# Batch 1's k turned by one DMA transpose instead of 64 PE transposes

## The chip, the core and the metric

The kernel runs on one core of a Trainium2 chip. The metric is the device time of one execution in microseconds, taken as the median of several runs. The core has five engines with a queue each, which run side by side and wait for one another through semaphores: TensorE (PE, with the weight loads PEld shown apart), VectorE (DVE), ScalarE (ACT), GpSimd (POOL) and SyncE (SP). POOL and SP also issue the DMA transfers; the 16 DMA engines work through POOL's transfers in a queue that the profile calls q0 and through SP's in one called q1.

## What is computed

An attention with 4 batches, 8 heads, 768 positions and head size 64, followed by a gated feed-forward layer with a gated residual. Each position attends to the positions closer than 16, and to one summary of each of the 24 blocks of 32 positions (the block's maximum of k and its mean of v).

```python
k_sum = k.reshape(B, H, nb, block, D).max(axis=3)
v_sum = v.reshape(B, H, nb, block, D).mean(axis=3)
scores_l = scale * q @ k.T, kept where abs(i - j) < window
scores_s = scale * einsum('bhsd,bhnd->bhsn', q, k_sum) + log(block)
a = softmax(concatenate([scores_l, scores_s]))
x = a @ concatenate([v, v_sum])            # then heads side by side: 3072 x 512
ffn = (gelu(x @ w_gate) * (x @ w_val)) @ w_out
out = x + sigmoid(x @ w_res) * ffn
```

## The kernel before

**Units.** The 3072 rows of x are worked through in eight units `u` of 384 rows: `u // 2` is the batch, `u % 2` its half. A unit's feed-forward part makes twelve tiles `gvT[:, fo]` (`fo` 0 to 11): four products into `g` with `w_gate`, four into `vv` with `w_val`, a gelu on ACT (L400) and a product on DVE (L401). Then `first_out` (unit 0) or `mid_out` weaves the output products `r` (L433) and `f` (L443) of unit u with the attention of unit u+1: `s_step` makes the scores of one head pair (L317) and their exponentials, `av_step` the weighted sum of v (L355), and `xt_step` or `xt_dma` turn the result for the next unit. The order of all instructions is written out by hand; each engine runs its own in that order.

**Layouts.** `s_step` wants k with the head dimension on the partitions: `kW[b % 2]` holds, for each of twelve 64-row tiles and four head pairs, 128 columns: 64 own keys, 32 keys of the neighbouring tiles (the rims, columns `QT:BAND`), and the 24 block maxima (`BAND:BAND + NB`). `k_blocks` makes the maxima (L237) and copies them to all tiles (L241) on DVE. `k_rims` copies the rims (L245, L246) on the engine that it is given. The two `kW` buffers alternate by batch.

**How k gets there.** Batches 0 and 1 are loaded by `load_k` into `k_sb` with eight positions to a row (long contiguous pieces), turned by 64 PE transposes into PSUM (`turn_pair`, L220), and placed by `k_place`: an ACT copy (L252), then `k_blocks` and `k_rims` on DVE, head pair by head pair. For batch 1 the load is issued on POOL's queue before unit 0's loop goes on, the transposes (`turn_all`) stand after fo 0 of unit 1, and the four `k_place` after fo 0, 2, 4 and 6. Batches 2 and 3 are loaded by `load_k_nat` into `k_nat` (one transfer for each head, 64 partitions by 12 tiles by 64 values), turned by a single DMA transpose on SP's queue (`turn_k`, L131) at fo 6 of the even unit before, with `k_rims` on POOL just behind it; `k_blocks` follow on DVE at fo 2 to 5 of the odd unit.

**What else stands on the queues there.** POOL, after the weights: the load of batch 1's k, eight loads of its v (`vext`, L107), six of its q (`q_nat`, L127). A load of POOL waits until the eighth load before it has landed. In unit 1 at fo 5, `turn_q` turns q by two DMA transposes on SP (L136), and `vsum_grp` makes the block means of v: PE products `vs` (L290), an ACT copy `vpart` (L294), four small transfers `vsum` issued by POOL (L296). Then POOL copies them to six of the twelve tiles with `vsum_bc` (L302, twice), and to the others in `mid_out`. SP has the three outputs of unit 0 (L456), the rims of v (`v_rims`, L113 and L114), the two q transposes, and later the `xt_dma` and outputs of unit 1.

In unit 0 the four `xt_step` take turns between two PSUM banks and are all copied out by ACT (L382); the fourth is `xt_step(0, 3, st, **o_turn)`.

Of the kernel before, what the change touches and what calls it, by code (L numbers as in the profile page):

```python
# [15 lines left out]
def kernel(  # L16
# [11 lines left out]
    nc = tc.nc  # L28
# [16 lines left out]
    NP = H // 2  # L45
# [15 lines left out]
    ps_o = ctx.enter_context(tc.tile_pool(name="ps_o", bufs=1, space=bass.MemoryType.PSUM))  # L61
# [25 lines left out]
    def load_k(b, t, i, n):  # L87
        hs = slice(i * H // n, (i + 1) * H // n)
        nc.gpsimd.dma_start(out=t[:, hs].rearrange("p h j d -> p h (j d)"),
                            in_=k[b, hs].rearrange("h (p j) d -> p h (j d)", j=PJ))  # L90

    def k_tile():
        return qk.tile([PP, H, PJ, D], BF16, tag="k_sb", name="k_sb")
# [11 lines left out]
    def v_loads(b):  # L105
        for h in range(H):
            nc.gpsimd.dma_start(out=vext[b % 2][0:QT, :, h, 0:D],  # L107
                                in_=v[b, h].rearrange("(t p) d -> p t d", p=QT))
# [7 lines left out]
    k_sb, q_sb = {}, {}  # L116

    def load_k_nat(b):
        k_nat = qk.tile([QT, NT, DM], BF16, tag="k_nat", name="k_nat")
        for h in range(H):  # L120
            nc.gpsimd.dma_start(out=k_nat[:, :, h * D:(h + 1) * D],
                                in_=k[b, h].rearrange("(t p) d -> p t d", p=QT))
        return k_nat

    def load_q_nat(b):
        for c in range(NQ):
            nc.gpsimd.dma_start(out=q_nat[:, c].rearrange("p (h d) -> p h d", d=D),  # L127
                                in_=q[b, :, c * 128:(c + 1) * 128, :].rearrange("h p d -> p h d"))

    def turn_k(b, k_nat):  # L130
        nc.sync.dma_start_transpose(out=kW[b % 2].rearrange("d t g k -> d (t g) k")[:, :, 0:QT],  # L131
                                    in_=k_nat.rearrange("p t f -> p (t f)"))
# [6 lines left out]
    with tc.manual_schedule():  # L139
# [76 lines left out]
        def turn_pair(src, hp, tp):  # L216
            n, _, nj, _ = src.shape
            for j in range(nj):
                for hh in range(2):
                    nc.tensor.transpose(tp[hh * 64:hh * 64 + 64, j, :], src[:, 2 * hp + hh, j, :],  # L220
                                        ident[0:n, 0:n])
            return tp

        def turn_tile(src, pool, tag):
            return pool.tile([128, src.shape[2], src.shape[0]], BF16, tag=tag, name="tp")

        def turn_all(src):
            n, _, nj, _ = src.shape
            s2 = ps_s.tile([128, 2, 1024], BF16, tag="s", name="tp")
            tps = [s2[:, i, 0:nj * n].rearrange("d (j p) -> d j p", j=nj) for i in range(2)]  # L230
            tps += [turn_tile(src, ps_t, "t"), turn_tile(src, ps_o, "ao")]
            return [turn_pair(src, hp, tps[hp]) for hp in range(NP)]

        def k_blocks(b, hp):
            kw = kW[b % 2][:, :, hp]
            ks = work.tile([128, NB], BF16, tag="ks", name="ks")
            nc.vector.tensor_reduce(  # L237
                out=ks.rearrange("d (t n) -> d t n", n=2),
                in_=kw[:, :, 0:QT].rearrange("d t (n w) -> d t n w", w=BLK),
                axis=mybir.AxisListType.X, op=ALU.max)  # L240
            nc.vector.tensor_copy(kw[:, :, BAND:BAND + NB], ks.unsqueeze(1).to_broadcast([128, NT, NB]))  # L241

        def k_rims(b, hps, eng):
            kw = kW[b % 2][:, :, hps]
            eng.tensor_copy(kw[:, 0:NT - 1, :, QT:QT + WIN], kw[:, 1:NT, :, 0:WIN])  # L245
            eng.tensor_copy(kw[:, 1:NT, :, QT + WIN:BAND], kw[:, 0:NT - 1, :, QT - WIN:QT])  # L246
# [4 lines left out]
        def k_place(b, hp, tp):  # L251
            nc.scalar.copy(kW[b % 2][:, :, hp, 0:QT].rearrange("d t (p j) -> d t p j", j=PJ),  # L252
                           tp.rearrange("d j (t p) -> d t p j", t=NT))
            k_blocks(b, hp)
            k_rims(b, slice(hp, hp + 1), nc.vector)
# [121 lines left out]
        def xt_step(u, ko, st, pool, tag, copy=nc.vector.tensor_copy):  # L377
            xp = pool.tile([128, TU], BF16, tag=tag, name="xp")
            for sub in range(NSUB):
                nc.tensor.transpose(xp[:, sub * 128:(sub + 1) * 128],  # L380
                                    st["xn"][:, ko, sub, :], ident[:])
            copy(st["xT"][:, ko, :], xp[:])  # L382
# [5 lines left out]
        def new_unit():  # L388
            return {"xn": upool.tile([128, KO, NSUB, 128], BF16, tag="xn", name="xn"),
                    "xT": upool.tile([128, KO, TU], BF16, tag="xT", name="xT")}  # L390


        def gv_mm(ps, w, st, fo, kos):
            for ko in kos:
                nc.tensor.matmul(ps[:, 0:TU], w[:, ko, fo * 128:(fo + 1) * 128], st["xT"][:, ko, :],  # L395
                                 start=(ko == 0), stop=(ko == KO - 1), skip_group_check=True)
# [82 lines left out]
        tk, tq, ao = {}, {}, {}  # L479
# [11 lines left out]
        st = new_unit()  # L491
# [44 lines left out]
        o_turn = dict(pool=ps_o, tag="ao", copy=nc.scalar.copy)  # L536
# [6 lines left out]
        def gv_part(fo, ko):  # L543
            gv_mm(gv[fo][0], w_gate, st, fo, (ko,))
            gv_mm(gv[fo][1], w_val, st, fo, (ko,))
# [2 lines left out]
        xt_step(0, 2, st, **t_turn)  # L548
        gv_part(0, 1)
        gv_mm(gv[1][0], w_gate, st, 1, (0, 1))  # L550
        xt_step(0, 3, st, **o_turn)
        gv_part(0, 2)
        gv_mm(gv[1][1], w_val, st, 1, (0, 1))
        gv_part(0, 3)
# [100 lines left out]
        for u in range(NU):  # L655
            b, half = u // 2, u % 2
            nb = b + 1
            if half == 0 and nb == 1:
                k_sb[nb] = k_tile()
                load_k(nb, k_sb[nb], 0, 1)  # L660
                v_loads(nb)
                load_q_nat(nb)
            if u:
                gvT = upool.tile([128, FO, TU], BF16, tag="gvT", name="gvT")
            for fo in range(0 if u else 2, FO):
                if u == 0 and fo == 2:
                    unit0_extras(fo)
                    continue
                if u > 1 and fo == 0:
                    fo_first(st, gvT)  # L670
                elif u and fo == FO - 2:
                    fo_last_two(st, gvT)
                elif u == 0 or fo < FO - 2:
                    fo_step(st, gvT, fo)
                if u == 0:
                    unit0_extras(fo)
                if u == 0 and fo == 9:
                    tq = turn_all(q_sb[1])
                if u == 0 and fo in (9, 10):
                    for hp in range(2 * fo - 18, 2 * fo - 16):  # L680
                        q_place(1, hp, tq[hp])
                if half == 0 and 1 < nb < B and fo == 0:
                    pool_after(st["xT"][0:1, KO - 1, 0:1])
                    k_nat = load_k_nat(nb)
                    v_loads(nb)
                if half == 0 and b and fo == 1:
                    v_rims(b, HT, NT)
                if half == 0 and 1 < nb < B and fo == 6:
                    turn_k(nb, k_nat)
                    k_rims(nb, slice(0, NP), nc.gpsimd)  # L690
                if half == 1 and nb < B:
                    if fo == 0:
                        v_rims(nb, 0, HT)
                        if nb > 1:
                            pool_after(st["xT"][0:1, KO - 1, 0:1])
                            load_q_nat(nb)
                    if fo == (5 if nb == 1 else 1):
                        turn_q(nb, 0)
                        turn_q(nb, 1)
                        vsum_grp(nb, ps_t, "t")  # L700
                        for i in range(2):
                            vsum_bc(nb, 3 * i, 3 * i + 3, nc.gpsimd)
                    if nb == 1:
                        if fo == 0:
                            tk = turn_all(k_sb[nb])
                        if fo in (0, 2, 4, 6):
                            hp = (2, 0, 1, 3)[fo // 2]
                            k_place(nb, hp, tk[hp])
                    elif 2 <= fo < 2 + NP:
                        k_blocks(nb, fo - 2)  # L710
            if u == NU - 1:
                last_out(u, st, gvT)
            else:
                nst = new_unit()
                (mid_out if u else first_out)(u, st, gvT, nst)
                st = nst

# [29 lines left out]
```

The softmax here doesn't subtract the row's maximum and nothing guards it: scores larger than these inputs give would overflow.

## Time and profile before

| | |
|---|---|
| median of 3 runs | 256.26 us (256.26 to 256.71) |
| the profiled execution | 256.39 us, of which its span is 254.6 us |
| granted TensorE clock | 0.998 |
| 64 transposes of batch 1's k on PE (L220) | 207 ns each, overlapping, start 53.04 us |
| ACT copies of k out of PSUM (L252, all 8) | 798 ns each |
| DVE rim copies, one head pair (L245, L246, all 8 each) | 217 and 215 ns |
| POOL rim copies, all head pairs (L245, L246, 2 each) | 816 and 1096 ns |
| issue to landing: k_sb of batch 1 / kW<-k_nat | 18.6 us / 9.5 us |

The span is what the trace covers; the run's time also has what lies around it. A line of a timeline gives the start, the length, the engine, the line of the kernel, the operation with output and input, the count, and in brackets how long the engine had been idle and what ended that. The lines of a DMA queue give the packets, the megabytes and the time of its packets as a share of 16 engines' time.

### The profile page before, as it was taken

What the parts mean: (1) busy time and instruction counts of PE and PEld (TensorE: products, weight loads), DVE (VectorE), ACT (ScalarE), POOL (GpSimd) and SP (SyncE); (2) the same over time, 40 slices, a digit from 0 to 9 for tenths busy, and PEclk for the clock granted to TensorE, in tenths of its full rate; (3) what the DMA queues carried; (4) which work ended last, traced back from release to release, by engine and by line L of the source; (5) the groups of instructions that cost most, each with busy time, mean ns of one, the idle gap of its engine ahead of it and who ended that gap; (6) DMA issues with size and microseconds to landing.
All of it is one profiled execution on the core that took longest, in us unless ns stands there. A gap on an engine that the chain in (4) does not pass through costs nothing.

```text
span 254.6 us, 5847 instructions
## 1 busy us (share of the span) xinstructions
PE 246.6 (97%) x2303; PEld 139.7 (55%) x2328; DVE 159.4 (63%) x364; ACT 129.6 (51%) x216; POOL 97.3 (38%) x128
## 2 busy tenths in 40 slices
PE   6999999999999999999999999999999999999994
PEld 2676555565545665446544665446545555456544
DVE  6985796397667544858567544958567544854424
ACT  8885468366572337353572337254572337353320
POOL 8895542361506970274406970274404000000000
PEclk9999999999999999999999999999999999999999
DMA  5999999999404999399404999289604400230003
GB/s 80 177 182 197 197 205 207 175 176 222 61 19 121 159 150 150 56 161 171 103 18 120 162 155 153 49 162 170 104 18 115 98 3 0 50 139 0 3 1 124
DMA packets 98107, 29.34 MB, mean 115 GB/s; under 512 B 83224, under 2 KB 94944, under 8 KB 97984
## 3 DMA queue, kind: packets, MB, share of 16 engines
q0 software_dynamic: 68352, 14.76, 66.3%
q1 hardware_dynamic: 29728, 14.21, 25.7%
q8 instruction: 18, 0.29, 0.5%
q14 instruction: 9, 0.07, 0.1%
HBM read 29.36 MB, written 6.29 MB: 140 GB/s over the span
## 4 chain that ended last, share of the span: by engine, by line
PE 93%; DVE 5%; issue 2%; DVEq 0%
PE g L395 25%; PE vv L395 24%; PE f L443 23%; PE r L433 8%; PE s L317 3%; PE ao L355 3%; PE vs L282 1%; PE ao L367 1%; PE tp L220 1%; PE vs L290 1%; DVE ks L237 1%; PE xp L380 1%; DVE o L452 1%; DVE th L449 1%; PE gv L395 1%
## 5 line engine op out<-in xcount | busy, mean ns | idle before, releaser
L401 DVE TENSOR_TENSOR gvT<-ge,vv 128x384 bf16<-128x384 f32 x95 | 52.2, 552 | 48.1 <-PE vv L395 43.9
L400 ACT ACTIVATE ge<-g 128x384 f32<-128x384 f32 x95 | 46.7, 491 | 67.3 <-DVE gvT L401 34.8
L395 PE MATMUL g<-xT,w_gate 128*128 128x384 bf16 x380 | 78.0, 326 | 0.0
L395 PE MATMUL vv<-xT,w_val 128*128 128x384 bf16 x380 | 77.8, 326 | 0.0
L443 PE MATMUL f<-w_out,gvT 128*128 128x512 bf16 x262 | 62.7, 379 | 1.5 <-issue 1.1
L395 PEld LDWEIGHTS <-w_gate 128*128 128x128 bf16 x384 | 37.1, 98 | 26.2 <-issue 1.4
L395 PEld LDWEIGHTS <-w_val 128*128 128x128 bf16 x384 | 37.6, 98 | 24.7
L443 PEld LDWEIGHTS <-gvT 128*128 128x128 bf16 x276 | 25.7, 98 | 29.5
L107 POOL DMA_DIRECT2D vext<-in_v_dram x32 | 24.1, 777 | 15.0 <-DMA w_out<-in_moe_w_out_dram 5.6
L436 ACT ACTIVATE th<-r 128x512 f32<-128x512 f32 x24 | 13.5, 607 | 27.6 <-PE r L433 27.6
L449 DVE SCALAR_TENSOR_TENSOR th<-th,f 128x512 f32<-128x512 f32 (+2 forms) x26 | 16.6, 640 | 14.4 <-PE f L443 14.4
L341 DVE TENSOR_TENSOR P<-P,maskt 128x768 bf16<-128x768 bf16 x28 | 16.2, 580 | 11.0 <-ACT P L337 6.1
L433 PE MATMUL r<-w_res,xT 128*128 128x512 bf16 x88 | 22.7, 380 | 0.4
L302 POOL COPY vext<-vsum 32x1536 bf16<-32x1536 bf16 x12 | 17.2, 1464 | 13.0 <-DMA vsum<-vpart 12.9
L452 DVE SCALAR_TENSOR_TENSOR o<-th,xn 128x512 f32<-128x512 f32 (+2 forms) x26 | 18.2, 701 | 0.9
L375 DVE TENSOR_TENSOR xn<-ao,rz 128x384 bf16<-128x384 f32 x32 | 17.8, 557 | 1.1
L337 ACT ACTIVATE P<-s,bias_t 128x768 bf16<-128x768 f32 x17 | 15.3, 901 | 4.5 <-PE s L317 4.3
L127 POOL DMA_DIRECT2D q_nat<-in_q_dram x18 | 15.8, 899 | 0.9 <-issue 0.7
L334 ACT ACTIVATE P<-s,bias_t 128x384 bf16<-128x384 f32 x30 | 15.7, 579 | 0.0
L237 DVE TENSOR_REDUCE ks<-kW 128x24 bf16<-128x768 bf16 x16 | 15.1, 943 | 0.0
L433 PEld LDWEIGHTS <-xT 128*128 128x128 bf16 x96 | 8.8, 98 | 9.9
L373 DVE RECIPROCAL rz<-ao 128x6 f32<-128x6 f32 x32 | 6.1, 191 | 10.9 <-PE ao L355 10.0
(90 smaller groups left out, 187.1 us busy)
## 6 DMA issues: line engine op xcount, KB each, us to landing
out_dram<-o SPq DMA_DIRECT2D x23, 256.0 KB, 2.2
vext<-in_v_dram POOLq DMA_DIRECT2D x32, 96.0 KB, 6.4
q_nat<-in_q_dram POOLq DMA_DIRECT2D x18, 128.0 KB, 6.4
w_gate<-in_moe_w_gate_dram POOLq DMA_DIRECT2D x6, 256.0 KB, 8.9
w_val<-in_moe_w_val_dram POOLq DMA_DIRECT2D x6, 256.0 KB, 9.3
w_out<-in_moe_w_out_dram POOLq DMA_DIRECT2D x3, 512.0 KB, 14.4
k_nat<-in_k_dram POOLq DMA_DIRECT2D x16, 96.0 KB, 5.8
vext<-vext SPq DMA_DIRECT2D x6, 144.0 KB, 5.4
```

The lines of the kernel that those rows point to most:

```text
L107: nc.gpsimd.dma_start(out=vext[b % 2][0:QT, :, h, 0:D], in_=v[b, h].rearrange("(t p) d -> p t d", p=QT))
L237: nc.vector.tensor_reduce(out=ks.rearrange("d (t n) -> d t n", n=2), in_=kw[:, :, 0:QT].rearrange("d t (n w) -> d t n w", w=BLK), axis=myb ...
L302: eng.tensor_copy(vext[b % 2][96:128, lo:hi, :, 0:D], src)
L341: nc.vector.tensor_mul(Pf, Pf, maskt.unsqueeze(1).to_broadcast([128, 2 * HT, QT]))
L375: nc.vector.tensor_mul(xn, ao[:, :, :, 0:D], rz.to_broadcast([128, NSUB, 2, D]))
L395: nc.tensor.matmul(ps[:, 0:TU], w[:, ko, fo * 128:(fo + 1) * 128], st["xT"][:, ko, :], start=(ko == 0), stop=(ko == KO - 1), skip_group_ch ...
L400: nc.scalar.activation(ge[:], g[:, 0:TU], AF.Gelu)
L401: nc.vector.tensor_mul(gvT[:, fo, :], ge[:], vv[:, 0:TU])
L433: nc.tensor.matmul(r[:], st["xT"][:, ko, ss], w_res[:, ko, :], start=(ko == 0), stop=(ko == KO - 1))
L443: nc.tensor.matmul(st["f", sub][:], gvT[:, fo, ss], w_out[:, fo, :], start=(fo == 0), stop=(fo == FO - 1), skip_group_check=True)
L449: nc.vector.scalar_tensor_tensor(th[:, cs], th[:, cs], 1.0, f[:, 0:n], ALU.add, ALU.mult)
L452: nc.vector.scalar_tensor_tensor(o.rearrange("p (k d) -> p k d", d=128), th[:, cs].rearrange("p (k d) -> p k d", d=128), 0.5, x, ALU.mult, ...
```

## The change

Batch 1's k is loaded by `load_k_nat` and turned by `turn_k`, as batches 2 and 3 are. The turn is issued in unit 0, ahead of `first_out`. `k_rims` goes to POOL at fo 6 of unit 1, and the four `k_blocks` follow on DVE at fo 6 to 9. The last `xt_step` of unit 0 is copied out by DVE (the default of `copy`) and no longer by ACT.

```diff
-        xt_step(0, 3, st, **o_turn)
+        xt_step(0, 3, st, ps_o, "ao")
...
             if half == 0 and nb == 1:
-                k_sb[nb] = k_tile()
-                load_k(nb, k_sb[nb], 0, 1)
+                k_nat = load_k_nat(nb)
                 v_loads(nb)
                 load_q_nat(nb)
...
                         vsum_grp(nb, ps_t, "t")
                         for i in range(2):
                             vsum_bc(nb, 3 * i, 3 * i + 3, nc.gpsimd)
-                    if nb == 1:
-                        if fo == 0:
-                            tk = turn_all(k_sb[nb])
-                        if fo in (0, 2, 4, 6):
-                            hp = (2, 0, 1, 3)[fo // 2]
-                            k_place(nb, hp, tk[hp])
-                    elif 2 <= fo < 2 + NP:
-                        k_blocks(nb, fo - 2)
+                    lead = 6 if nb == 1 else 2
+                    if nb == 1 and fo == lead:
+                        k_rims(nb, slice(0, NP), nc.gpsimd)
+                    if lead <= fo < lead + NP:
+                        k_blocks(nb, fo - lead)
...
                 nst = new_unit()
+                if u == 0:
+                    turn_k(nb, k_nat)
                 (mid_out if u else first_out)(u, st, gvT, nst)
```

The functions that it now calls for batch 1, as they were:

```python
def load_k_nat(b):
    k_nat = qk.tile([QT, NT, DM], BF16, tag="k_nat", name="k_nat")
    for h in range(H):
        nc.gpsimd.dma_start(out=k_nat[:, :, h * D:(h + 1) * D],
                            in_=k[b, h].rearrange("(t p) d -> p t d", p=QT))
    return k_nat

def turn_k(b, k_nat):
    nc.sync.dma_start_transpose(out=kW[b % 2].rearrange("d t g k -> d (t g) k")[:, :, 0:QT],
                                in_=k_nat.rearrange("p t f -> p (t f)"))

def k_rims(b, hps, eng):
    kw = kW[b % 2][:, :, hps]
    eng.tensor_copy(kw[:, 0:NT - 1, :, QT:QT + WIN], kw[:, 1:NT, :, 0:WIN])
    eng.tensor_copy(kw[:, 1:NT, :, QT + WIN:BAND], kw[:, 0:NT - 1, :, QT - WIN:QT])
```

## The prediction

> **What bounds the kernel now.** I read the page's busy shares first, then the chain that ended last, then the timeline of the stretch that the change touches (50 to 72 us) engine by engine, then the DMA queues in short windows. The first two say that TensorE sets the time:
>
> ```profile
> PE 246.6 (97%) x2303; PEld 139.7 (55%) x2328; DVE 159.4 (63%) x364; ACT 129.6 (51%) x216; POOL 97.3 (38%) x128
> ...
> PE 93%; DVE 5%; issue 2%; DVEq 0%
> ```
>
> So whatever shortens or delays PE's queue shows in the end time one for one. PE's timeline (start, length, what, count) around the removed transposes, with lines between left out:
>
> ```profile
> 53.04 1.55 PE L220 MATMUL tp<-ident,k_sb 96*64 96x96 bf16 x64
> 54.52 0.82 PE L395 MATMUL g<-xT,w_gate 128*128 128x384 bf16 x4
> ...
> 61.13 0.83 PE L290 MATMUL vs<-vext,bgrp 64*32 64x512 bf16 x12
> ...
> 69.79 0.52 PE L317 MATMUL s<-qT,kW 64*128 64x64 bf16 x24
> ```
>
> The 64 transposes occupy PE itself; nothing covers them. Everything from 54.5 to 69.8 is back to back. The next reader of batch 1's k is the score step at 69.79. POOL's timeline for the same stretch, and the two rim copies where they stand for batch 2:
>
> ```profile
> 30.07 1.01 POOL L89 DMA_DIRECT2D k_sb<-in_k_dram  x1 [0.59 <-DMA w_val<-in_moe_w_val_dram]
> ...
> 48.96 0.75 POOL L107 DMA_DIRECT2D vext<-in_v_dram  x1 [3.15 <-DMA k_sb<-in_k_dram]
> ...
> 62.88 2.04 POOL L296 DMA_DIRECT2D vsum<-vpart  x4 [7.67 <-ACT vpart L294]
> 67.53 2.88 POOL L302 COPY vext<-vsum 32x1536 bf16<-32x1536 bf16 x2 [2.60 <-DMA vsum<-vpart]
> ...
> 103.29 0.86 POOL L245 COPY kW<-kW 128x704 bf16<-128x704 bf16 x1 [8.33 <-DMA kW<-k_nat]
> 104.10 1.09 POOL L246 COPY kW<-kW 128x704 bf16<-128x704 bf16 x1
> ```
>
> POOL waits 2.60 us for the vsum transfer and ends the two L302 copies at 70.41, after the score step has begun: today nothing on PE needs them then. SP's queue, whose first instruction is an output at 52.69, and the k transpose of batch 2:
>
> ```profile
> 52.69 2.98 SPq L456 DMA_DIRECT2D out_dram<-o  x3
> 55.99 0.61 SPq L113 DMA_DIRECT2D vext<-vext  x1
> ...
> 57.35 6.34 SPq L136 DMA_TRANSPOSE qT<-q_nat  x2
> ...
> 93.70 5.81 SPq L131 DMA_TRANSPOSE kW<-k_nat  x1
> ```
>
> Last, the queues (packets, MB, share of 16 engines) in the 3 us from 153.8, which begin 3.6 us after batch 3's k transpose was issued at 150.22:
>
> ```profile
> q1 hardware_dynamic: 1975, 0.51, 100.0%
> q0 software_dynamic: 149, 0.02, 18.8%
> ```
>
> In 150 to 152 q0, the queue of POOL's loads, moved 2368 packets, some 1180 a us; beside the transpose it moves 50 a us. Batch 2's shows the same (93 packets from 96.8 to 99.8). The last v load behind each transpose took 8.7 and 8.8 us to land instead of about 5.8.
>
> **What the Trainium skill says.** "DMA: Bandwidth & Descriptors", Specifications, gives 512 B as the least transfer for full rate. The trace agrees in direction: the 1 KB rows of w_out and k_sb move at 209 GB/s (44 to 46 us), the 128 B rows of v at 155 (48 to 52). The same page, Queues, rings and completion order, says that each DMA engine round-robins between queues packet by packet; the freeze just shown is much worse than an even share, so I price from the trace. "TensorE: Matmul & The Clock Gate", Part 1, says that an idle window of about 3.4 us halves PE's clock for at least one window more; no gap here is that long (granted clock 0.998).
>
> **The change part by part**, on the span of the profiled run (254.6 us; the run took 256.39, the median of the runs is 256.26, so a shift of the span is added to either).
>
> *Removed from PE.* 64 transposes: the chain of waits gives them 1.48 us, and the first product after them 0.76 in place of 0.65: -1.59. Four ACT copies (0.79) and eight DVE rim copies (0.20 and 0.19) go too; ACT and DVE are behind PE there, so 0.
>
> *The copy of xT moved from ACT to DVE (unit 0).* ACT took 0.48, DVE's same form 0.36; DVE is idle from 21.9 to 23.9 and PE has a gap before 23.03: -0.12. If PE's gap has another cause, 0.
>
> Without a new wait the score step would start at 69.79-1.71 = 68.08.
>
> *k_nat's loads.* Eight transfers of 768 packets for one of 768 long ones. POOL issues each only when the eighth before it has landed, which w_out sets until 45 us. On the DMA engines: 6144 packets at about 1200 a us are 5.1 us, where k_sb's 768 at 205 a us were 3.75: everything behind is 1.4 us later. k_sb landed at 48.67; k_nat's last at about 50.2.
>
> *The transpose on SP.* Now SP's first instruction. Issued at 50.2 it holds SP until 56.0 (5.81), so the outputs of unit 0 go at 56 to 59 instead of 52.7 to 55.7, the rims after them, and the q transpose at 60 or later. The outputs' buffers are next needed some 20 us later: 0. It lands 9.5 us after issue (both times before): 59.7, in time for DVE's first block maximum at about 62. But from 52.8 to 56.7 it freezes q0, which then holds v's last load and all six of q_nat. v should land at 59 to 60, and the vs products would start at 59.42: wait 0 to 0.5, I take 0.3. Of q_nat's 6144 packets I leave 270 to the first half microsecond after v, at a rate halved by the transpose's tail; 5874 are left at 58.6. With the outputs beside it q0 moved some 730 a us before (54 to 60 us), so it ends at 65.5 to 66 (6 us at 730, the rest at some 1150; before: 61).
>
> *DVE.* Maximum and copy (0.94+0.24) per head pair now stand at fo 6 to 9, beside a product of 0.55 in each 1.30 us of PE: 0.44 us of backlog each, 1.8 in all, gone within the last two fo and the score step. Cost 0 as long as PE waits longer for POOL.
>
> *The rims move to POOL, behind L302.* This decides. The instruction order has vsum's four issues, the two L302, then L245 and L246; the first score matmuls wait for L245 and L246, and PE runs in order: all of unit 1's r and f products and unit 2 are queued behind. Step by step: vs at 59.7 (61.13-1.71+0.3); vsum issues start 1.75 later, as before, and last 2.04: 61.5 to 63.5. The wait for the landing is the unknown. Least: the 2.60 of before, so L302 at 66.1. Most: vsum is behind q_nat in q0 and the q transpose freezes q0 again: 70. In the later units, where q_nat is just ahead, the wait was 5.57 and 4.70. With q_nat ending near 65.7 and about 2 us to the last landing, I take 68.0. L302 twice is 2.88: 70.9. L245 and L246 are 1.90 at batch 2: 72.85. The score step starts at 72.9, so +3.1 against 69.79. After it PE is as packed as before, and the later units keep their distances.
>
> Sum: -1.59-0.12+4.8 of waiting = +3.1; 256.39+3.1 = 259.5 profiled, 259.4 for the median.
>
> **The rivals.**
> *Short wait.* The freeze falls between loads and vsum lands as fast as before: L302 at 65.8 to 66.1, score step at 70.7 to 71.0, about +0.9: 257.2. For: vsum is four tiny transfers. Against: q_nat is later by 1.4 us and a freeze of 4.
> *Long wait and cold clock.* q_nat is thrown further back or the q transpose (needed by the same score step) lands last; L302 at 69 to 70 and a gap over 5 us, in which an idle window fits; half clock for one window costs up to 1.7 (estimate from the TensorE page's section). +4 to +7, about 261.5. For: the queue is full until 66. Against: PE does other work until 68.
> *Faster.* The rims are ready by 68.08 and the saving stays: 256.26-1.7 = 254.6. It needs L302 to start by 63.3, when POOL has hardly issued the fourth vsum transfer; only if the waits of the score step do not cover the rims, or POOL takes the rims earlier. It decides as soon as L246 ends before 68.1. Against it stands POOL's order.
> That the change does not do what it says: the transposes leave PE's queue altogether, so this is none.
>
> **How the numbers follow.** Forecast 0.55 (its own range 257.9 to 260.6), short wait 0.17, long wait 0.20, faster 0.08. The range 257.0 to 261.8 leaves out the faster case, the least of the short waits (0.03) and the upper third of the long ones (0.07). About 0.2% (0.5 us) is what a measurement here can tell from no change: the faster case gives 0.06 to faster and 0.02 to same, the shortest waits 0.03 to same, the rest is slower: 0.06, 0.05, 0.89.
>
> **What would show it.** Right: no L220 from k_sb after 50 us; L131 as SP's first instruction near 50; L302 starting near 68 behind a wait for vsum, L245 and L246 right after; PE idle 4 to 5 us before L317, released by POOL L246; the later units equally long. Wrong: PE waiting at L317 for the q transpose, or stalled earlier at L290 for v by over 1 us (then vsum's price was mine in the wrong place); no gap at all (the order on POOL does not bind); a granted clock below 1.0 after the gap (long wait).

## The result and the profile after

| | before | after |
|---|---|---|
| median of 4 runs each | 256.49 us (256.26 to 257.12) | 263.31 us (262.66 to 264.45) |
| ratio | 1 | 1.0267, 95% interval 1.0225 to 1.0309 |
| the profiled execution | 256.39 us, span 254.6 | 264.45 us, span 262.4 |
| granted TensorE clock | 0.998 | 0.985 (the other runs 0.984, 0.993, 0.987) |
| first score product of unit 2 that has all it needs (L317) | 69.79 us | 75.11 us |

The change costs 6.8 us at the median and 8.1 in the profiled run (7.8 of them in the span): slower, as forecast, but more than twice as much, and above the range. Medians and ratios here are over fast runs; one run of experiment 2 (266.83 us) was a slow one and is left out. The page of after, in its clock line over 40 slices and in its shares of the chain that ended last:

```profile
PEclk9999999999968999999999999999999999999999
...
PE 69%; DMA 21%; POOL 5%; issue 2%; DVE 1%; POOLq 0%; DVEq 0%
```

Before, PE had 93% of that chain, and the clock line is all nines. Now transfers and POOL stand in it. The 21% of DMA aren't a cost of that size: from POOL the chain leads back through vsum and q_nat into the loads of the first 45 us, which ran before as well. In one place, slices 12 and 13 (72 to 85 us), the clock is down. PE's timeline of after in that stretch:

```profile
53.23 0.81 PE L395 MATMUL g<-xT,w_gate 128*128 128x384 bf16 x4 [0.20 <-DVE th L449]
...
60.55 0.83 PE L290 MATMUL vs<-vext,bgrp 64*32 64x512 bf16 x12 [0.64 <-DMA q_nat<-in_q_dram]
...
74.39 0.23 PE L317 MATMUL s<-qT,kW 64*128 64x64 bf16 x2 [5.11 <-POOL kW L245]
75.11 0.77 PE L317 MATMUL s<-qT,kW 64*128 64x64 bf16 x22 [0.48 <-POOL kW L246]
75.81 3.60 PE L433 MATMUL r<-w_res,xT 128*128 128x512 bf16 x8
...
80.85 0.57 PE L355 MATMUL ao<-vext,P 128*64 128x65 bf16 x24
```

The last of these lines, as it was before:

```profile
72.94 0.57 PE L355 MATMUL ao<-vext,P 128*64 128x65 bf16 x24
```

The 64 transposes are gone, and the score step comes 5.3 us later instead of 1.7 earlier. The gap in front of L317 (5.11 + 0.48 us) ends when POOL ends the two rim copies. What follows is slow too: from the score step to the first `ao` products took 5.7 us (75.11 to 80.85), where the same work took 3.15 before (69.79 to 72.94). This second loss, 2.6 us, goes with the clock (experiment 2 tests it); the table of busy time by stretch (PE's, PEld's, DVE's, ACT's and POOL's busy us, then the clock, the DMA share and GB/s) has it in its third column from the end:

```profile
69.00:72.00 3.00, 0.29 (x2) 0.00 (x0) 1.26 (x4) 0.82 (x1) 1.36 (x1) 1.00 1.00 141
73.00:74.00 1.00, 0.00 (x0) 0.00 (x0) 0.00 (x0) 0.00 (x0) 0.94 (x2) 0.89 0.14 29
74.00:77.00 3.00, 2.13 (x27) 1.15 (x28) 0.47 (x1) 1.40 (x3) 1.05 (x2) 0.50 0.00 0
77.00:80.00 3.00, 3.00 (x8) 1.06 (x7) 0.65 (x2) 1.60 (x3) 0.00 (x0) 0.50 0.00 0
80.00:81.00 1.00, 1.00 (x12) 0.30 (x12) 0.00 (x0) 0.04 (x1) 0.00 (x0) 0.70 0.00 0
```

The clock falls to half late in the gap, near 73.8, and comes back near 80.6 (0.89 and 0.70 are means over a microsecond in which it changes). 5.3 + 2.6 = 7.9 us, and the span is 7.8 longer: the same `g` products in the loop that follows start at 92.79 for 84.89, and later units keep their distances. So all of the loss arises between 50 and 81 us. Next POOL's timeline of after:

```profile
62.30 1.54 POOL L296 DMA_DIRECT2D vsum<-vpart  x3 [5.05 <-ACT vpart L294]
64.41 0.50 POOL L296 DMA_DIRECT2D vsum<-vpart  x1 [0.56 <-DMA q_nat<-in_q_dram]
70.64 2.87 POOL L302 COPY vext<-vsum 32x1536 bf16<-32x1536 bf16 x2 [5.73 <-DMA vsum<-vpart]
73.57 0.77 POOL L245 COPY kW<-kW 128x704 bf16<-128x704 bf16 x1
74.28 0.76 POOL L246 COPY kW<-kW 128x704 bf16<-128x704 bf16 x1
```

The rims need nothing but kW, which the k transpose had filled by 61.5 (issue 50.19, 11.3 us to landing). They start 12 us after that, behind L302 and its wait for vsum, 5.73 us where it was 2.60. Why vsum is late is seen in SP's timeline of after and in the packets:

```profile
50.19 5.68 SPq L131 DMA_TRANSPOSE kW<-k_nat  x1
55.92 1.58 SPq L456 DMA_DIRECT2D out_dram<-o  x3
...
64.93 6.96 SPq L136 DMA_TRANSPOSE qT<-q_nat  x2
```

The DMA queues of after (packets, MB, share of 16 engines), first from 53 to 56 us:

```profile
q1 hardware_dynamic: 1435, 0.37, 87.4%
q0 software_dynamic: 141, 0.02, 9.4%
```

and then from 62 to 63 us:

```profile
q1 hardware_dynamic: 167, 0.31, 92.7%
q0 software_dynamic: 165, 0.02, 31.7%
```

In the first stretch, beside the k transpose, q0 moved 141 packets; before, in the same 3 us:

```profile
q0 software_dynamic: 2843, 0.36, 189.3%
```

In the second the outputs of unit 0, moved behind the transpose, left q0 165 a us. At 64.93 the q transpose is issued, and q0 falls once more: 361 and 475 packets in 65 to 67, after 1221 in 64 to 65. The last packets of q_nat and vsum move between 68 and 69; L302 starts at 70.64.

### The profile page after: what moved, and what is told of

Its sections match the earlier page's. It is cut to its first block, busy times and chain, and to the rows that moved or that the text cites. A ratio compares the mean times of both kernels' runs of the same rounds, so it can differ in the third digit from the quotient of the medians.

```text
span 262.4 us, 5748 instructions
## 1 busy us (share of the span) xinstructions
PE 250.8 (96%) x2264; PEld 139.4 (53%) x2264; DVE 157.5 (60%) x357; ACT 126.3 (48%) x211; POOL 104.4 (40%) x137
## 4 chain that ended last, share of the span: by engine, by line
PE 69%; DMA 21%; POOL 5%; issue 2%; DVE 1%; POOLq 0%; DVEq 0%
PE f L443 20%; PE g L395 18%; PE vv L395 18%; PE r L433 8%; DMA w_out<-in_moe_w_out_dram 6%; DMA q_nat<-in_q_dram 4%; DMA w_val<-in_moe_w_val_dram 4%; DMA vext<-in_v_dram 3%; DMA vsum<-vpart 2%; PE ao L355 2%; POOL vext L107 2%; DMA k_sb<-in_k_dram 2%; PE s L317 2%; DVE o L452 1%; DVE th L449 1%
## 5 line engine op out<-in xcount | busy, mean ns | idle before, releaser
L401 DVE TENSOR_TENSOR gvT<-ge,vv 128x384 bf16<-128x384 f32 x95 | 52.1, 552 | 48.7 <-PE vv L395 45.8
L443 PE MATMUL f<-w_out,gvT 128*128 128x512 bf16 x276 | 65.3, 383 | 0.0
L341 DVE TENSOR_TENSOR P<-P,maskt 128x768 bf16<-128x768 bf16 x28 | 15.7, 560 | 16.7 <-ACT P L337 11.5
L449 DVE SCALAR_TENSOR_TENSOR th<-th,f 128x512 f32<-128x512 f32 (+2 forms) x26 | 16.6, 639 | 14.3 <-PE f L443 14.3
L433 PE MATMUL r<-w_res,xT 128*128 128x512 bf16 x96 | 24.8, 401 | 0.0
L121 POOL DMA_DIRECT2D k_nat<-in_k_dram x24 | 18.6, 806 | 10.7 <-DMA w_out<-in_moe_w_out_dram 5.8
L302 POOL COPY vext<-vsum 32x1536 bf16<-32x1536 bf16 x12 | 17.2, 1463 | 14.0 <-DMA vsum<-vpart 13.8
L237 DVE TENSOR_REDUCE ks<-kW 128x24 bf16<-128x768 bf16 x16 | 15.1, 943 | 0.0
## 6 DMA issues: line engine op xcount, KB each, us to landing
out_dram<-o SPq DMA_DIRECT2D x23, 256.0 KB, 2.3
w_gate<-in_moe_w_gate_dram POOLq DMA_DIRECT2D x6, 256.0 KB, 9.0
w_val<-in_moe_w_val_dram POOLq DMA_DIRECT2D x6, 256.0 KB, 9.4
```

Of the source, the lines that this page charges most:

```text
L121: nc.gpsimd.dma_start(out=k_nat[:, :, h * D:(h + 1) * D], in_=k[b, h].rearrange("(t p) d -> p t d", p=QT))
L302: eng.tensor_copy(vext[b % 2][96:128, lo:hi, :, 0:D], src)
L401: nc.vector.tensor_mul(gvT[:, fo, :], ge[:], vv[:, 0:TU])
L433: nc.tensor.matmul(r[:], st["xT"][:, ko, ss], w_res[:, ko, :], start=(ko == 0), stop=(ko == KO - 1))
L443: nc.tensor.matmul(st["f", sub][:], gvT[:, fo, ss], w_out[:, fo, :], start=(fo == 0), stop=(fo == FO - 1), skip_group_check=True)
L449: nc.vector.scalar_tensor_tensor(th[:, cs], th[:, cs], 1.0, f[:, 0:n], ALU.add, ALU.mult)
```

## Experiments

The first theory: the score step's wait is POOL's order (rims behind L302), and the clock adds its part after the gap. The rival: what comes late is the data (kW or the q transpose), and POOL only stands last in the records.

**1. The rims ahead of L302.**

```diff
                         vsum_grp(nb, ps_t, "t")
+                        if nb == 1:
+                            k_rims(nb, slice(0, NP), nc.gpsimd)
                         for i in range(2):
                             vsum_bc(nb, 3 * i, 3 * i + 3, nc.gpsimd)
...
-                    if nb == 1 and fo == lead:
-                        k_rims(nb, slice(0, NP), nc.gpsimd)
```

> The changed kernel with the two rim copies of batch 1 put ahead of the two L302 copies on POOL; nothing else differs. Theory (POOL's order keeps the rims behind the landing of vsum): the rims are done by 65 us, and the first score matmul of unit 2 waits for the next thing in line, the first q transpose, which landed at 70.9 us in the changed kernel; it starts near 71.0, the gap is 2.3 us, too short for the clock to drop, and the time is about 257.7 us. Rival (the DMA queue alone is late and POOL's order adds nothing): the score step still starts at 74 to 75 us and the time stays near 263.

Measured: 257.26 us (9 runs), ratio to before 1.0046 (1.0018 to 1.0073), clock 1.0. POOL's timeline of this run:

```profile
64.00 0.78 POOL L245 COPY kW<-kW 128x704 bf16<-128x704 bf16 x1
64.72 0.78 POOL L246 COPY kW<-kW 128x704 bf16<-128x704 bf16 x1
70.24 2.88 POOL L302 COPY vext<-vsum 32x1536 bf16<-32x1536 bf16 x2 [4.74 <-DMA vsum<-vpart]
```

and PE's:

```profile
66.11 0.81 PE L395 MATMUL vv<-xT,w_val 128*128 128x384 bf16 x4 [0.57 <-DVE gvT L401]
...
70.59 0.53 PE L317 MATMUL s<-qT,kW 64*128 64x64 bf16 x24 [0.78 <-DMA qT<-q_nat]
```

L302 still waits for vsum until 70.24, and it no longer matters: six of the 6.8 us are gone with the order of two instructions, the clock's share among them, as the long gap is gone too. The score step came near the expected 71.0, and the rival is out. What is late next is the q transpose, issued at 64.42 and 6.1 us to its landing. The new stall on gvT comes up again below.

**2. The gap kept, but filled.** 22 products on a constant tile before the score step, so that PE isn't idle while it waits.

```diff
         def mid_out(u, st, gvT, nst):
             n = u + 1
             other = dict(pool=ps_t, tag="t")
+            if u == 1:
+                keep_warm(22)
```

> The changed kernel with 22 matmuls on a tile of zeros put on PE ahead of the first score step of unit 2, 4.8 us of work that fits into the gap. Theory (the gap of 5.5 us also costs a half clock from 73.9 to 80.7 us): the score step starts at 75.1 us as before, the clock stays at 1.0, and the time is 2.6 us less, about 260.7 us. Rival (the slow stretch after the gap is the products waiting for something else): no gain, or a loss, 263 to 264 us.

Measured: ratio 1.0206 (1.0189 to 1.0224), 261.56 us in the profiled run. PE's timeline of this run:

```profile
68.48 4.91 PE L475 MATMUL wp<-warm 128*128 128x512 bf16 x22
...
74.93 0.49 PE L317 MATMUL s<-qT,kW 64*128 64x64 bf16 x22 [0.51 <-POOL kW L246]
75.35 1.90 PE L433 MATMUL r<-w_res,xT 128*128 128x512 bf16 x8
```

The score step starts only 0.18 us earlier than in after, but eight `r` products take 1.90 us instead of 3.60, and the profiled run is 2.9 us shorter; between the medians (263.31 and 261.66) it is about 1.6. So of after's loss some 1.6 to 2.7 us (the 2.9 less the 0.18) are the clock, and the rest is the wait.

**3. The order on POOL alone, in the kernel before.** k is turned on PE as it was; only batch 1's rims move to POOL, behind L302.

```diff
             k_blocks(b, hp)
-            k_rims(b, slice(hp, hp + 1), nc.vector)
+            if b == 0:
+                k_rims(b, slice(hp, hp + 1), nc.vector)
...
                             k_place(nb, hp, tk[hp])
+                        if fo == 6:
+                            k_rims(nb, slice(0, NP), nc.gpsimd)
```

> The kernel before, with batch 1's k loaded and turned by PE as it was, and only its rim copies taken from DVE and given to POOL behind the two L302 copies. Theory: L302 ends at 70.4 us as before, the rims at 72.3, the score step starts at 72.35 instead of 69.8, the gap of 2.5 us is too short for the clock to drop, and the time is 259.0 us. Rival (POOL's place costs nothing without the DMA's lateness): 256.4 us.

Measured: 260.14 us (258.06 to 260.6, 4 runs), ratio 1.0129 (1.0087 to 1.0171). PE's timeline of the profiled run, which is the one of 258.06 us (lines are one further down here):

```profile
70.92 0.20 PE L318 MATMUL s<-qT,kW 64*128 64x64 bf16 x2 [1.02 <-POOL kW L245]
71.63 0.49 PE L318 MATMUL s<-qT,kW 64*128 64x64 bf16 x22 [0.51 <-POOL kW L246]
```

With no DMA transpose of k at all, the order costs 1.7 us in this run, which is its excess over before. The other three runs took 259.89 to 260.6 us at a clock of 0.991, for 1.0 here: 0.009 of 258 us is 2.3 us, about as much as they are longer (1.8 to 2.5). So the expectation that such a gap is too short for the clock failed in three runs of four. Only the profiled run has a trace, so how long their gap was stays open. Before ran at 0.986 and 0.987 in two of the 28 runs of that round (259.63 and 259.56 us): a lower clock comes there too, but rarely.

**4. The transpose alone, in the kernel before.** A DMA transpose of batch 1's k into a tile that nobody reads, as SP's first instruction there.

```diff
                 nst = new_unit()
+                if u == 0:
+                    scr = qk.tile([128, NT * DM], BF16, tag="k_nat", name="scr")
+                    nc.sync.dma_start_transpose(out=scr[:, 0:32 * PP].rearrange("d (c p) -> d c p", p=PP),
+                                                in_=k_sb[1].rearrange("p h j d -> p (h j d)"))
```

> The kernel before, with one added DMA transpose as SP's first instruction: it turns the loaded k_sb of batch 1 into a scratch tile that nothing reads (as many bytes as the change's transpose); k itself is still turned by PE. It shows what the transpose does to the transfers beside it. Theory: POOL's queue stands still for some 4 us from 51.5 us; v lands at 58 to 59, q at 65 to 66 instead of 62.2, vsum 2 to 4 us later than before; the q transpose lands at about 69, so the time rises by 0 to 1 us, to 256.4 to 257.5. Rival (the transpose is nearly free for the other queue, and the lateness of the changed kernel comes from the smaller rows of k's load): q lands by 63 us and the time is unchanged.

Measured: 256.64 us (20 runs), ratio 1.0001 (0.9976 to 1.0025). The DMA queues of this run from 53 to 56 us:

```profile
q1 hardware_dynamic: 1597, 0.41, 82.8%
q0 software_dynamic: 790, 0.10, 50.3%
```

q0 is held back (790 packets for 2843), the q loads take up to 14 us to land, and the q transpose is issued at 65.32 instead of 57.35. POOL's and PE's lines of this run:

```profile
69.28 2.87 POOL L302 COPY vext<-vsum 32x1536 bf16<-32x1536 bf16 x2 [4.41 <-DMA vsum<-vpart]
...
69.81 0.53 PE L317 MATMUL s<-qT,kW 64*128 64x64 bf16 x24
```

L302 waits 4.41 us in place of 2.60, and the score step still starts at 69.81 for 69.79: the delays end just before it (the q transpose lands at 69.77). So the transpose's harm to other transfers is real and, by itself, free; in the runs here it turns into time only through what is made to wait behind vsum, or through a score step that could come early and finds q_nat's transpose late.

**5. Unit 0's outputs out of the way.** In after, the three outputs are issued on SP behind the q transposes instead of ahead of the v rims.

```diff
-            nc.sync.dma_start(out=out[row:row + 128, cs], in_=o[:])
+            if u:
+                nc.sync.dma_start(out=out[row:row + 128, cs], in_=o[:])
+            else:
+                late.append((row, cs, o))
...
                         turn_q(nb, 1)
+                        for row, cs, o in late:
+                            nc.sync.dma_start(out=out[row:row + 128, cs], in_=o[:])
+                        late.clear()
```

> The changed kernel with the three output transfers of unit 0 issued on SP behind the two q transposes instead of behind the k transpose; POOL's order is the changed kernel's, rims last. Theory (vsum lands late because q_nat is behind the freeze of the transpose and then shares the engines with 0.79 MB of outputs from 60.5 to 63.5 us): the last of q lands some 3 us earlier, L302 starts at 67.5 instead of 70.6, the score step at 72.0 instead of 75.1, and the time is 259 us, or 260.5 where the clock still drops. Rival (only the freeze matters): no more than 1 us earlier, 262 to 263 us.

Measured: 262.5 us, ratio 1.0233 (1.0217 to 1.0249), where the rival had put it. The last q load lands 4.8 us earlier (at 64.72, for 69.56; all six take 7.9 to 8.7 us). Part of that are the outputs, which no longer stand beside them. Part is chance: at 58.6 us, before the outputs had begun to move in after, q0 had 5921 packets left here for 7163 there. And part is that the q loads now end before the q transpose freezes them. But that transpose goes 3.5 us earlier as well, at 61.47, and meets vsum. The DMA queues of this run from 64 to 67 us:

```profile
q1 hardware_dynamic: 1626, 0.41, 107.0%
q0 software_dynamic: 113, 0.02, 6.1%
```

and POOL's timeline:

```profile
68.95 2.87 POOL L302 COPY vext<-vsum 32x1536 bf16<-32x1536 bf16 x2 [5.10 <-DMA vsum<-vpart]
```

L302 gains 1.7 us, not the 4.8 of the loads: the second freeze is what sets vsum's landing. The score step comes at 73.42:

```profile
73.42 0.77 PE L317 MATMUL s<-qT,kW 64*128 64x64 bf16 x22 [0.47 <-POOL kW L246]
```

The gap of 4.09 + 0.47 us still halves the clock (0.985 over the span).

**6 and 7. Both together.** Experiments 1 and 5 in one kernel, and then also block maxima from fo 5 on (`lead = 5`).

> Both: rims ahead of the L302 copies on POOL, and the outputs of unit 0 behind the q transposes on SP. Theory: nothing that the score step needs is behind vsum any more, and the first q transpose lands at 67 to 68 us instead of 70.5; the score step starts at 68.5 to 69.0, held up by DVE's backlog of block maxima (0.9 us in the run with the rims first), and the time is 255.5 to 256.0 us. Rival (the freeze alone sets q): q lands at 70 as before and the time stays at 257.2.

> As the run with both, and the four block maxima on DVE start one fo earlier (fo 5 to 8 instead of 6 to 9). Theory (DVE's backlog stalls PE by 0.9 us at fo 9 to 11): the last products of unit 1 run back to back again, the score step starts at 68.2, and the time is 255.0 us, below the kernel before. Rival (DVE then waits for the transpose, which landed at 61.1 to 61.5, and holds the products up instead): 256 us.

Measured: 256.55 us (12 runs), ratio 1.0002 (0.9991 to 1.0014), and 256.61 us (13 runs), 1.0010 (1.0001 to 1.0020). The first undoes all of the loss, but isn't below before, as expected of it (255.5 to 256.0). The second was expected to win another 1.5 us; the score step stands at 69.61 in it, near the q transpose's landing (61.64 + 7.0 = 68.6) but not at it, behind the same stall on gvT as in experiment 1. DVE's timeline of the second kernel says what holds gvT:

```profile
62.19 0.24 DVE L241 COPY kW<-ks 128x288 bf16<-128x288 bf16 x1
...
63.79 1.68 DVE L241 COPY kW<-ks 128x288 bf16<-128x288 bf16 x1
65.38 0.54 DVE L401 TENSOR_TENSOR gvT<-ge,vv 128x384 bf16<-128x384 f32 x1
```

and POOL's beside it:

```profile
63.88 0.78 POOL L245 COPY kW<-kW 128x704 bf16<-128x704 bf16 x1
64.59 0.78 POOL L246 COPY kW<-kW 128x704 bf16<-128x704 bf16 x1
```

The same copy takes 0.24 us once and 1.68 the next time, and it ends 0.1 us after POOL's second rim copy (65.47 and 65.37). In experiments 1 and 6 it is the same: 1.75 and 1.74 us, each ending 0.1 us after L246. The Trainium skill, "SBUF — State Buffer", section "SBUF: two separate sides", says that a pair of ports is shared by GpSimd and those VectorE operations that run in a two-port mode or have two inputs in SBUF, as an exclusive lock: the first to start holds it for its whole instruction while the other fully blocks. The trace agrees in the effect: the copy is held to POOL's end rather than slowed by a share. In the records it begins 0.1 to 0.2 us before POOL's copy, so which of the two was first can't be read from them. Here it was held over both rim copies. In experiment 6 the last of these copies met the two L302 and got in between them: it took 0.54 us and ended at 70.99, 0.1 us after the first. The masks (L341, two inputs in SBUF) are held in the same way, in experiment 7 beside an L302 that runs to 71.86:

```profile
71.16 1.11 DVE L341 TENSOR_TENSOR P<-P,maskt 128x768 bf16<-128x768 bf16 x1 [0.81 <-ACT P L337]
```

The same one before:

```profile
71.33 0.56 DVE L341 TENSOR_TENSOR P<-P,maskt 128x768 bf16<-128x768 bf16 x1 [0.81 <-ACT P L337]
```

Not every DVE instruction is held: in experiment 6 a block maximum (L237) and two gvT products (L401, one input in PSUM) beside L302 kept their lengths, 0.95 us and 1.00 for the two. So it is a matter of the operation, not of DVE as a whole.

**8. The copy of xT alone.** Only the last `xt_step` of unit 0 is copied out by DVE; everything else as before.

> The kernel before with the last xT copy of unit 0 on DVE instead of ACT, nothing else. Theory: the copy is 0.12 us shorter and PE's first unit starts 0.1 us earlier, which the rounds can hardly tell: 256.3 to 256.5 us. Rival (DVE is the busier engine in unit 0 and the copy delays a product): 256.7 or more.

Measured: 256.52 us, ratio 1.0003 (0.9994 to 1.0013). No effect on the time that can be told from none; 0.12 us would be too small for it. In the traces it shows: the `g` product that reads this copy follows its predecessors by 0.49 us here and in after (22.46 to 22.95), and by 0.57 before (22.46 to 23.03), so the copy won 0.08 us.

**9 and 10. The rims on ACT.** If the shared ports are the cause of the stall, the same copies on ACT must not bring it. One rim copy each at fo 6 and 7, on ACT, first in after and then in the kernel of experiment 7.

```diff
-                    if nb == 1 and fo == lead:
-                        k_rims(nb, slice(0, NP), nc.gpsimd)
+                    if nb == 1 and fo in (6, 7):
+                        k_rim(nb, slice(0, NP), fo - 6, nc.scalar.copy)
```

> Only change to the kernel after: batch 1's two rim copies stand on ACT, one in each of feature blocks 6 and 7, instead of on POOL behind the vsum copies. If POOL's place behind vsum is what holds the score step, it is released by the q transpose now, which was issued at 64.4 and took 6.1 us in the run with the rims moved ahead on POOL: score step near 70.6, time 257.2 (between 256.7 and 257.6). DVE's block copy (L241) stays at 0.23 us in every instance, since no POOL copy runs beside it, and PE has no stall of over 0.3 us on gvT before the score step. Rival: the 1.7 us instance of the block copy was queueing behind the reductions, not POOL: it comes back, with the stall of 0.57 us.

> The version with outputs behind the q transposes and block maxima from feature block 5, with the rims on ACT instead of POOL. If POOL's copies stretched DVE's block copy from 0.23 to 1.7 us and with it PE by 0.87 us, the block copy stays at 0.23 us and the score step comes 0.8 to 0.9 us earlier than the 69.6 there: 68.7, near the landing of the q transpose; time 255.7 against 256.6 there and 256.4 before, which is the first version to beat the kernel before. Rival: DVE's queue of maxima and gvT products or ACT's two extra copies cost the same stall elsewhere, and the time stays at 256.5.

Measured: 257.63 us (8 runs), ratio 1.0039 (1.0025 to 1.0053), and 257.72 us (256.23 to 259.51, 14 runs), 1.0045 (1.0024 to 1.0066). ACT's timeline of the second:

```profile
62.26 0.77 ACT L252 COPY kW<-kW 128x704 bf16<-128x704 bf16 x1
...
63.56 0.77 ACT L250 COPY kW<-kW 128x704 bf16<-128x704 bf16 x1
```

DVE's timeline of the same kernel, beside the second of these:

```profile
64.05 0.24 DVE L241 COPY kW<-ks 128x288 bf16<-128x288 bf16 x1
```

and PE's:

```profile
69.63 0.53 PE L323 MATMUL s<-qT,kW 64*128 64x64 bf16 x24 [0.65 <-DMA qT<-q_nat]
```

DVE's block copy runs beside ACT's rim copy (63.56 to 64.33) in 0.24 us; the other three take 0.23 to 0.24 as well, and PE has no stall on gvT in either kernel. So the stretching belongs to POOL, not to the tile that all three write. But the time isn't won: PE now waits 0.65 us for the q transpose, issued at 62.35 here and at 61.64 in experiment 7. In the first of the two kernels that wait is 1.86 us (score step at 70.73). And in the second, vsum comes 1.0 us later than in experiment 7 (L302, which is L308 in this kernel, starts at 69.97 for 68.98), so that the first `ao` products wait for it:

```profile
73.23 0.79 PE L361 MATMUL ao<-vext,P 128*64 128x65 bf16 x19 [0.16 <-POOL vext L308]
73.95 0.52 PE L323 MATMUL s<-qT,kW 64*128 64x64 bf16 x24
```

In experiment 7 that second score step stands at 73.27. Both expected times were missed (257.2 and 255.7). Why the second scatters over 3 us, and has a median 1.1 above experiment 7, while its profiled span is only 0.2 longer, isn't settled. No version that was run beats the kernel before; experiment 6 equals it.

## Why the prediction was wrong in size

The direction and the mechanism held: the order on POOL decides (experiments 1 and 3), and the gap in front of L317 looks as forecast, released by L245 and L246. What came was the rival called "long wait and cold clock", at the upper end of its +4 to +7 by the medians and above it in the profiled run. The sum missed in two terms.

| term, profiled run | predicted | measured |
|---|---|---|
| transposes and xT copy removed, at fo 1's `g` | -1.71 | -1.29 (54.52 to 53.23) |
| wait of vs for the loads | 0.3 | 0.64 |
| first vsum issue | 61.5 | 62.30 |
| L302 starts | 68.0 (66.1 to 70) | 70.64 |
| L245 + L246 | 1.90 | 1.47 |
| score step | 72.9 | 75.11 |
| clock | 0 in the forecast, up to 1.7 in the rival | 2.6 (1.6 between the medians of after and experiment 2) |
| sum | +3.1 | +8.1 (7.8 in the span) |

*The step that failed first* is "With q_nat ending near 65.7 and about 2 us to the last landing, I take 68.0". The 2 us held: vsum's last transfer landed at 70.47, about 2 us after the last packets, and L302 started at 70.64. q_nat's end did not: its last packets moved between 68 and 69, some 3 us late. Two amounts in the packets make up 2.2 us of that.

The first is the queue's length. The prediction let the freeze find "v's last load and all six of q_nat" in q0, 6912 packets at 52.8 us. In after 7829 data packets of v and q moved from then on: a bit more than two loads of v still stood there, not one. The freeze let through about as many as was priced (910 had moved by 58.6, for 1038 in the prediction's own count), so 6919 were left at 58.6 in place of 5874. The 1045 more are 0.9 us at the 1150 a us of a free queue. That isn't an accident of one run: the traced versions of the changed kernel all had 8069 to 8112 packets (with vsum's and the short ones that mark an end) left in q0 at 52.8.

The second is the second freeze, named in the prediction for its upper end only: 836 packets in 65 to 67, where 2300 would have gone, 1.3 us. The outputs, which look like a third cause, were priced rightly: they moved at 0.3 MB a us in 61 to 63 and left q0 213 and 165 packets, but over the six microseconds from 58.6 q0 moved 4455, 740 a us for the 730 that were assumed.

Experiment 5 shows how the causes trade places: without the outputs the last q load lands 4.8 us sooner, and vsum only 1.7, because the q transpose moves up into it. vsum sits between q_nat, the first half of which releases the q transpose, and the q transpose, which freezes vsum. This loop is why the freeze couldn't be added up as one delay. The prediction had a measure of it: in the later units, where q_nat is just ahead, it read waits of 5.57 and 4.70 us, and it took 4.5 (63.5 to 68.0); what came was 5.73.

*The step that failed second* is the clock, left out of the forecast because the gap was put at 4 to 5 us and a gap of over 5 us was wanted for it. It was 5.6. The Trainium skill, "TensorE: Matmul & The Clock Gate", Part 1, from which one window at half clock was priced, has the mechanism right for this case: after's clock falls at the end of the gap. The size was too small. Half clock lasted from about 73.8 to 80.6, 6.8 us or two windows of 3.4, and it cost 2.6 us, not 1.7. A gap of 4.6 us (experiment 5) brings it as well, again for 6.8 us, so it belonged in the forecast itself. There the clock fell 2.9 us after PE's last product had ended (68.6 to 71.5; the ends of products are modelled), in after 4.5 us; the first is less than the page's window of about 3.4. From what gap on the clock drops isn't settled by these runs: in experiment 3 it was lower in three runs whose gaps weren't traced.

*The removed work* gave 0.4 us less than the sum said. That "nothing covers them" was wrong: the transposes themselves had covered a wait of PE for DVE (L449) at fo 1's `g`, 0.20 us of idle, which with the run-out of the products before it moves the start by 0.35. The copy of xT gave 0.08 of its 0.12 (experiment 8).

*k's own transfer* was later than priced, landing at 61.5 rather than 59.7 (11.3 us, not 9.5), with no effect: the first block maximum starts at 63.37.

*DVE's block maxima at cost 0* was right while POOL's gap covers them: the last is done by 69.4. The condition that the prediction set, "as long as PE waits longer for POOL", was needed: with the rims ahead (experiment 1), the maxima and the held copy stall PE by 0.57 us.

*Outputs 20 us from being needed: 0* was right for their buffers, and their bytes were charged rightly in q0's 730 packets a us.

## What to carry to other kernels

Price a moved instruction by what stands ahead of it in its queue: here two copies of 0.77 us cost 6 us because they were put behind a wait that had nothing to do with them, and one move of two lines took it back. Count what a queue still holds when a freeze begins: here one load of v was assumed and two were there. Where a transfer is hemmed in by others that trigger each other, look at where the same pattern stood before (here the longer waits of the later units) rather than at the middle. And when a gap of PE is forecast at about the length that lowers its clock, put the clock into the forecast.

## What was not expected of the hardware

- DVE's copy of 288 elements to a row took 1.68 to 1.75 us instead of 0.24 while POOL ran two copies, and was unaffected by the same copies on ACT. It cost PE 0.57 us directly. Beside POOL's L302 the masks are held as well (1.11 us for 0.56), the maxima and gvT products are not.
- One DMA transpose of 768 rows of k (0.79 MB) as SP's first transfer leaves POOL's queue 78, 0, 63 and 116 packets a us in 53 to 57, for 686 to 1135 before. Where it stands alone (experiment 4) it leaves 90 to 412 and costs no time. How hard it freezes differs between runs: from 52.8 to 58.6 q0 moved 927 packets in after and 2174 in experiment 5, though SP had issued the same transfers up to the transpose.
- Half clock lasted 6.8 us after a gap of 5.6 us (after) and of 4.6 (experiment 5) alike, and cost 2.6 us in after's profiled run. The kernel with only the rims moved (experiment 3) had a lower clock, 0.991, in three of its four runs, which were 1.8 to 2.5 us longer than the fourth.
